# Linear attention and a gated FFN in one kernel: attention pieces issued on a fixed grid of ticks, with FFN matmuls between them

## The chip, the core and the metric

The kernel runs on one core of one Trainium2 chip. The metric is device time in microseconds (us) of one execution. In the profile PE is TensorE's matmuls, PEld its weight loads, DVE VectorE, ACT ScalarE, POOL GpSimd, SP SyncE. POOL and SP also issue the loads and stores. The kernel keeps its tiles in SBUF; its matmuls write to tiles in PSUM, of which it has five for attention (`pa` in the views) and three for the FFN (`pf`).

## The reference, cut to what matters

```python
# batch 8, heads 8, sequence 576, head size 64, 128 features; FFN 512 -> 1536 -> 512
def phi(x):
    proj = einsum('bhsd,df->bhsf', x, w_phi)
    proj = proj - max(abs(proj), axis=-1, keepdims=True)
    return concatenate([exp(proj), exp(-proj)], axis=-1)
q_p, k_p = phi(q), phi(k)
kv  = einsum('bhsf,bhsd->bhfd', k_p, v)
num = einsum('bhsf,bhfd->bhsd', q_p, kv)
den = einsum('bhsf,bhf->bhs', q_p, sum(k_p, axis=2)) + 1e-6
x   = (num / den)                       # heads joined: 4608 tokens x 512
out = (maximum(x @ w_gate, 0) * (x @ w_val)) @ w_out
```

A sequence of 576 is four chunks of 128 rows and 64 more. Both kernels put the last 64 rows of two batches together into one "mixed" tile of 128 rows.

## The kernel before

One attention unit takes two heads of one batch through the whole chain, K and Q together. PE transposes K and Q; DVE copies the result to SBUF; PE projects; DVE takes the maxima; ACT takes the exps; POOL scales v; PE forms kv; PE forms the numerators; DVE combines them; POOL divides; PE transposes the result for the FFN.

```python
def attn_unit(u, qn, kn, vn, mixed, kvs, xT):
    kpm, vs_m = mixed
    # ... (blk: one 128x128 block of K or Q)
    tT = transposed([blk(kn, i) for i in range(4)] + [blk(qn, i) for i in range(4)])
    kps, ek = k_features(tT[:, 0:4], "kp", sb_f)      # PE, DVE max, ACT exps
    vs = sb_f.tile([P, 8, 2, E], BF16, name="vs")
    scale_v(vs, ..., ek, slice(0, P))                 # POOL, two products of 1.04 us
    yield
    # ... q_features: PE, DVE max, ACT exps; cq = exp(2 m)
    yield
    # ... kv: 20 matmuls of 65 columns, ACT copies the result
    yield
    xu = sb_f.tile([P, 8, D], BF16, name="xu")
    for lo, n in GROUPS:                              # 3, 3 and 2 of 8 blocks
        # ... numerators (PE), then finish_rows: DVE t, u, 1/u; POOL x = u/den
    yield
    x_transposed(xu, xT[:, u, :].rearrange("p (c t) -> p c t", t=P))
```

The FFN of the batch before is a second generator. It is advanced by one step for each `yield` of attention. A step is a val and a gate product (8 matmuls) or one output tile (12 matmuls). The program order is only a proposal: the framework's scheduler may reorder the instructions.

```python
for b in range(B):
    # ... loads of the next batch
    ffn = ffn_group(b - 1, xT) if b else iter(())
    xT = sb_x.tile([P, NDC, SF], BF16, name="xT")
    for _ in attention(b, loaded, mix, state, xT):
        next(ffn, None)
    for _ in ffn:
        pass
for g, x in ((B - 1, xT), (B, xT_mix)):
    for _ in ffn_group(g, x):
        pass
```

Of the kernel before, what the change touches and what calls it, by code (L numbers as in the profile page):

```python
# [8 lines left out]
FP32 = mybir.dt.float32  # L9
# [7 lines left out]
def kernel(  # L17
# [16 lines left out]

    nc = tc.nc
# [18 lines left out]
    sb_mix = ctx.enter_context(tc.tile_pool(name="sb_mix", bufs=2))  # L54
    sb_T = ctx.enter_context(tc.tile_pool(name="sb_T", bufs=3))
    sb_f = ctx.enter_context(tc.tile_pool(name="sb_f", bufs=3))
    sb_kv = ctx.enter_context(tc.tile_pool(name="sb_kv", bufs=14))
# [7 lines left out]
    ident = singles.tile([P, P], BF16)  # L65
    make_identity(nc, ident)

    w2 = singles.tile([P, 2, F], BF16)
    nc.vector.memset(w2, 0.0)
    nc.gpsimd.dma_start(out=w2[0:D, 0, :], in_=w_phi)  # L70
    nc.gpsimd.dma_start(out=w2[D : 2 * D, 1, :], in_=w_phi)

    wg_sb = singles.tile([P, NDC, DFF], BF16)
    wv_sb = singles.tile([P, NDC, DFF], BF16)
    wo_sb = singles.tile([P, NFC, DM], BF16)
    xT_mix = singles.tile([P, NDC, SF], BF16)

    vsm = []
    for i in range(2):
        pair = []  # L80
        for bb in range(2):
            t = singles.tile([P, H, 2, E], BF16, name=f"vsm{i}{bb}")
            nc.vector.memset(t[SM * (1 - bb) : SM * (2 - bb)], 0.0)
            pair.append(t)
        vsm.append(pair)
# [8 lines left out]
    def load_batch(b, pieces):  # L94
        qn = sb_in.tile([P, H, C, D], BF16, name="qn")
        kn = sb_in.tile([P, H, C, D], BF16, name="kn")
        vn = sb_in.tile([P, H, C, D], FP32, name="vn")
        step = H // pieces
        for h in range(0, H, step):
            hs = slice(h, h + step)  # L100
            for t, src, eng in ((kn, k, nc.gpsimd), (vn, v, nc.sync), (qn, q, nc.gpsimd)):
                eng.dma_start(
                    out=t[:, hs],
                    in_=src[b, hs, 0:SF, :].rearrange("h (p c) d -> p h c d", c=C),
                )
        return qn, kn, vn

    def load_mixed(i):
        qm = sb_mix.tile([P, H, D], BF16, name="qm")
        km = sb_mix.tile([P, H, D], BF16, name="km")  # L110
        vm = sb_mix.tile([P, H, D], FP32, name="vm")
        for t, src, eng in ((km, k, nc.gpsimd), (vm, v, nc.sync), (qm, q, nc.gpsimd)):
            for bb in range(2):
                eng.dma_start(
                    out=t[SM * bb : SM * (bb + 1)],
                    in_=src[2 * i + bb, :, SF:S, :].rearrange("h p d -> p h d"),
                )
        return qm, km, vm

    def load_weights():  # L120
        nc.gpsimd.dma_start(out=wv_sb, in_=moe_w_val.rearrange("(c p) n -> p c n", p=P))
        nc.gpsimd.dma_start(out=wg_sb, in_=moe_w_gate.rearrange("(c p) n -> p c n", p=P))
        nc.gpsimd.dma_start(out=wo_sb, in_=moe_w_out.rearrange("(c p) n -> p c n", p=P))

    def transposed(blocks):

        pt = psum_a(BF16)
        n = len(blocks)
        for i, blk in enumerate(blocks):
            nc.tensor.matmul(  # L130
                pt[:, P * i : P * i + P], lhsT=blk, rhs=ident, is_transpose=True
            )
        t = sb_T.tile([P, 8, P], BF16, name="tT")
        nc.vector.tensor_copy(  # L134
            t[:, 0:n].rearrange("p a b -> p (a b)"), pt[:, 0 : P * n]
        )
        return t

    def project_rows(T2):

        pp = psum_a()
        for i in range(2):
            nc.tensor.matmul(  # L143
                pp[:, 2 * F * i : 2 * F * (i + 1)],
                lhsT=T2[:, i, :],
                rhs=w2.rearrange("p a f -> p (a f)"),
            )
        return pp

    def row_max(dst, pp):  # L150
        nc.vector.tensor_reduce(  # L151
            dst,
            pp.rearrange("p (c f) -> p c f", f=F),
            axis=AX.X,
            op=ALU.max,
            apply_absolute_value=True,
        )

    def k_features(kT, name, pool):

        mk = sb_s.tile([P, 8], FP32, name="mk")
        kps = []
        for i in range(2):
            pp = project_rows(kT[:, 2 * i : 2 * i + 2])
            row_max(mk[:, 4 * i : 4 * i + 4], pp)
            kp = pool.tile([P, 2, 4, F], BF16, name=f"{name}{i}")
            for s, sign in ((0, 1.0), (1, -1.0)):
                nc.scalar.activation(
                    kp[:, s].rearrange("p c f -> p (c f)"), pp, AF.Exp, scale=sign
                )  # L170
            kps.append(kp)
        ek = sb_s.tile([P, 2, 8], FP32, name="ek")
        for s, sign in ((0, -1.0), (1, 1.0)):
            nc.scalar.activation(ek[:, s, :], mk, AF.Exp, scale=sign)
        return kps, ek

    def scale_v(dst, src, ek, rows):

        for s in range(2):
            e = ek[rows, s, :]  # L180
            nc.gpsimd.tensor_tensor(  # L181
                dst[rows, :, s, 0:D],
                src[rows],
                e[:, :, None].to_broadcast([e.shape[0], 8, D]),
                op=ALU.mult,
            )
            nc.gpsimd.tensor_copy(dst[rows, :, s, D], e)  # L187

    def q_features(qT, m_slices, name):

        for i in range(2):
            pp = project_rows(qT[:, 2 * i : 2 * i + 2])
            row_max(m_slices[i], pp)
        qp = sb_f.tile([P, 2, 2, 4, P], BF16, name=name)
        for par in range(2):
            pf = psum_a()
            nc.tensor.matmul(  # L197
                pf, lhsT=w2[:, par, :], rhs=qT.rearrange("p a b -> p (a b)")
            )
            for s, sign in ((0, 1.0), (1, -1.0)):  # L200
                nc.scalar.activation(  # L201
                    qp[:, s, par].rearrange("p a b -> p (a b)"), pf, AF.Exp, scale=sign
                )
        return qp

    def finish_rows(parts, cq, xu, lo, n):

        t = sb_s.tile([P, 3, E], FP32, name="t")
        u = sb_s.tile([P, 3, E], FP32, name="u")
        r = sb_s.tile([P, 3, 1], FP32, name="r")  # L210
        for rows, pn in parts:
            ab = pn.rearrange("p (c s e) -> p c s e", s=2, e=E)[rows]
            np_ = ab.shape[0]
            nc.vector.tensor_tensor(  # L214
                t[rows, 0:n],
                ab[:, 0:n, 1],
                cq[rows, lo : lo + n][:, :, None].to_broadcast([np_, n, E]),
                op=ALU.mult,
            )
            nc.vector.tensor_tensor(u[rows, 0:n], ab[:, 0:n, 0], t[rows, 0:n], op=ALU.add)  # L220
        nc.vector.reciprocal(r[:, 0:n], u[:, 0:n, D : D + 1])  # L221
        nc.gpsimd.tensor_tensor(  # L222
            xu[:, lo : lo + n],
            u[:, 0:n, 0:D],
            r[:, 0:n].to_broadcast([P, n, D]),
            op=ALU.mult,
        )

    def x_transposed(xu, dst):
        pt = psum_a(BF16)  # L230
        for i in range(4):
            nc.tensor.matmul(  # L232
                pt[:, P * i : P * i + P],
                lhsT=xu[:, 2 * i : 2 * i + 2].rearrange("p a d -> p (a d)"),
                rhs=ident,
                is_transpose=True,
            )
        nc.vector.tensor_copy(dst, pt[:, 0:512].rearrange("p (a b) -> p a b", b=P))

    GROUPS = ((0, 3), (3, 3), (6, 2))  # L240

    def attn_unit(u, qn, kn, vn, mixed, kvs, xT):
        kpm, vs_m = mixed
        blk = lambda t, i: t[:, 2 * u + i // 2, 2 * (i % 2) : 2 * (i % 2) + 2, :].rearrange(
            "p c d -> p (c d)"
        )
        tT = transposed([blk(kn, i) for i in range(4)] + [blk(qn, i) for i in range(4)])
        kps, ek = k_features(tT[:, 0:4], "kp", sb_f)
        vs = sb_f.tile([P, 8, 2, E], BF16, name="vs")
        scale_v(  # L250
            vs, vn[:, 2 * u : 2 * u + 2].rearrange("p h c d -> p (h c) d"), ek, slice(0, P)
        )
        yield
        mq = sb_s.tile([P, 4, 2], FP32, name="mq")
        qp = q_features(tT[:, 4:8], [mq[:, :, hh] for hh in range(2)], "qp")
        cq = sb_s.tile([P, 8], FP32, name="cq")
        nc.scalar.activation(
            cq, mq.rearrange("p c h -> p (c h)"), AF.Exp, scale=2.0
        )
        yield  # L260
# [136 lines left out]
    for b in range(B):  # L397
# [6 lines left out]
        for _ in ffn:  # L404
            pass
# [35 lines left out]
```

## Time and profile before

| | before |
|---|---|
| time | 582.89 us (median of 3, 582.74 to 582.99) |
| span in the profile | 581.4 us |
| PE, DVE, ACT, POOL busy | 77, 48, 43, 30% |
| dense FFN matmuls begin | about 84 us |
| attention ends, FFN alone | from about 520 us |
| one batch in between | 61.9 us |

First the page of before: the busy time of each engine, then three rows of the view in 40 slices (a digit is the busy share of a slice in tenths; PEclk is the granted clock), then the shares of the chain of work that ended last ("issue" is time in which the engine waited for nothing that the profile shows).

```profile
PE 447.6 (77%) x3307; PEld 238.8 (41%) x3368; DVE 280.8 (48%) x681; ACT 248.5 (43%) x573; POOL 176.4 (30%) x317
...
PE   1315669896589788878789698966897788879996
...
POOL 6923322233622332233523222325222222210000
PEclk9999759999999969999899699998899799999999
...
PE 39%; POOL 19%; issue 15%; DVE 10%; ACT 10%; DMA 7%; POOLq 0%; DVEq 0%; another core or an unknown queue 0%; ACTq 0%
```

No engine is full. PE is low at the start, saturated only in the last slices, where the FFN runs alone, and rises and falls in between. Also, PE's busy time overstates its work. The Trainium skill ("Perfetto Trace Analysis", § Identifying the Most-Contended Engine) warns that matmul busy time is no good measure of how close a kernel is to the roofline, because pipelined instructions look smaller in the trace. Here they look longer than the time they take from PE, as the timeline of before shows. Columns: start, length, engine, line, operation, shapes, count.

```profile
308.89 2.75 PE L357 MATMUL pf<-wo_sb,h_3136 128*128 128x512 bf16 x12
```

Twelve matmuls take 2.75 us. Each is recorded with 0.379 us, so they start (2.75 - 0.379) / 11 = 0.2155 us apart. The FFN has 1296 of them, which is 279.5 us. Attention's shorter matmuls, read in the same way, add about 113 us. PE's work is therefore about 393 us of the 581.4.

Next, five rows of the view of waits of before: who waited for whom, us in total, times, longest.

```profile
ACT val_sb L349 <- PE pf L340: 122.5, 68, 6.3
POOL xu L222 <- DVE r L221: 116.8, 46, 5.8
...
PE pa L272 <- POOL vs L187: 55.9, 56, 5.6
...
PE pa L232 <- POOL xu L222: 35.4, 32, 8.0
...
POOL km L114 <- DMA wo_sb<-in_moe_w_out_dram: 6.5, 1, 6.5
```

ACT's and POOL's idle time costs nothing by itself. PE's does: PE stood 55.9 us for the scaled v and 35.4 us for POOL's x. The engines wait for each other in turn.

The pace of a batch is read from the weight loads of the output products, one group per batch. Columns: duration in ns (min/median/max), first and last start in us.

```profile
L357 PEld LDWEIGHTS <-h_1547 x48: 95/98/98, 180.9 to 193.7; 128*128 128x128 bf16 x48
...
L357 PEld LDWEIGHTS <-h_4725 x48: 95/98/98, 428.4 to 441.3; 128*128 128x128 bf16 x48
```

Four batches lie between these two: (428.4 - 180.9) / 4 = 61.9 us per batch. PE's work per batch is about 45.2 us.

### The profile page before, as it was taken

How to read it: one execution, taken by the hardware profiler on the slowest of the kernel's cores; microseconds unless marked ns; L12 is line 12 of the kernel's file. 1: busy time of each engine (PE TensorE's matmuls, PEld its weight loads, DVE VectorE, ACT ScalarE, POOL GpSimd, SP SyncE). 2: the span in 40 equal slices, each digit the busy share in tenths (PEclk: the TensorE clock that was granted, in tenths of full speed). 3: DMA queues.
4: the chain of work that ended last, by engine and by line, in shares of the span. 5: the costliest groups of instructions: out<-in, count | busy, mean ns of one | idle time of the engine just before them, and what ended most of it. 6: DMA issues, size and time to landing. Idle time of an engine off the chain costs nothing.

```text
span 581.4 us, 8833 instructions
## 1 busy us (share of the span) xinstructions
PE 447.6 (77%) x3307; PEld 238.8 (41%) x3368; DVE 280.8 (48%) x681; ACT 248.5 (43%) x573; POOL 176.4 (30%) x317
## 2 busy tenths in 40 slices
PE   1315669896589788878789698966897788879996
PEld 0213444453354444444345344533444444434442
DVE  3213556535664456538563555356543565373140
ACT  2303345534555445444453455345444454432331
POOL 6923322233622332233523222325222222210000
PEclk9999759999999969999899699998899799999999
DMA  9999160029200720082002700270001000100103
GB/s 202 206 203 105 12 135 1 1 62 165 28 1 19 129 72 1 19 163 47 1 1 72 147 0 2 63 156 1 1 19 56 0 2 4 71 1 1 72 1 72
DMA packets 45834, 33.63 MB, mean 58 GB/s; under 512 B 14048, under 2 KB 40160, under 8 KB 45792
## 3 DMA queue, kind: packets, MB, share of 16 engines
q0 software_dynamic: 27952, 14.19, 18.7%
q1 hardware_dynamic: 17840, 18.88, 10.2%
q8 instruction: 26, 0.43, 0.3%
q14 instruction: 16, 0.13, 0.1%
HBM read 37.81 MB, written 9.44 MB: 81 GB/s over the span
## 4 chain that ended last, share of the span: by engine, by line
PE 39%; POOL 19%; issue 15%; DVE 10%; ACT 10%; DMA 7%; POOLq 0%; DVEq 0%; another core or an unknown queue 0%; ACTq 0%
PE pf L340 15%; PE pf L357 12%; POOL vs L181 10%; DMA wo_sb<-in_moe_w_out_dram 5%; PE pa L272 4%; POOL xu L222 3%; DVE u L220 3%; DVE t L214 2%; DVE mk L151 2%; PE pa L232 2%; PE pa L130 2%; DMA kn<-in_k_dram 2%; ACT qp L201 2%; PE pa L143 2%; POOL vs L187 2%
## 5 line engine op out<-in xcount | busy, mean ns | idle before, releaser
L349 ACT CAST val_sb<-pf 128x512 bf16<-128x512 f32 x108 | 64.0, 598 | 129.2 <-PE pf L340 122.5
L340 PE MATMUL pf<-xT,wg_sb 128*128 128x512 bf16 x366 | 107.2, 392 | 5.2 <-ACT val_sb L349 2.7
L340 PE MATMUL pf<-xT,wv_sb 128*128 128x512 bf16 x359 | 110.0, 391 | 1.4 <-issue 0.4
L181 POOL TENSOR_TENSOR vs<-vn,ek 128x512 bf16<-128x512 f32 x64 | 66.8, 1043 | 138.0 <-issue 71.2
L222 POOL TENSOR_TENSOR xu<-u,r 128x192 bf16<-128x192 f32 (+1 forms) x108 | 48.9, 471 | 154.9 <-DVE r L221 116.8
L201 ACT ACTIVATE qp<-pa 128x512 bf16<-128x512 f32 x144 | 75.9, 630 | 19.6 <-PE pa L197 19.4
L214 DVE TENSOR_TENSOR t<-pa,cq 128x195 f32<-128x195 f32 (+3 forms) x120 | 36.7, 327 | 97.2 <-PE pa L286 91.0
L340 PEld LDWEIGHTS <-wg_sb 128*128 128x128 bf16 x432 | 41.8, 101 | 43.5 <-issue 6.8
L143 PE MATMUL pa<-w_96,tT 128*128 128x256 bf16 x288 | 50.1, 308 | 8.8 <-DVE tT L134 7.8
L340 PEld LDWEIGHTS <-wv_sb 128*128 128x128 bf16 x432 | 40.9, 101 | 37.3 <-issue 6.1
L232 PE MATMUL pa<-ident,xu 128*128 128x128 bf16 x144 | 26.1, 240 | 36.4 <-POOL xu L222 35.4
L151 DVE TENSOR_REDUCE mk<-pa 128x4 f32<-128x512 f32 x72 | 46.7, 686 | 14.1 <-PE pa L143 14.1
L365 ACT COPY out_sb<-pf 128x512 f32<-128x512 f32 x36 | 21.4, 593 | 65.9 <-PE pf L357 63.9
L134 DVE COPY tT<-pa 128x1024 bf16<-128x1024 bf16 (+1 forms) x40 | 25.4, 635 | 45.9 <-PE pa L130 45.7
L151 DVE TENSOR_REDUCE mq<-pa 128x4 f32<-128x512 f32 x64 | 41.0, 682 | 3.5 <-PE pa L143 3.5
L143 PEld LDWEIGHTS <-tT 128*128 128x128 bf16 x288 | 28.0, 108 | 32.1 <-DVE tT L134 21.3
L220 DVE TENSOR_TENSOR u<-pa,t 128x195 f32<-128x195 f32 (+3 forms) x120 | 37.2, 332 | 1.7 <-DVE r L221 0.4
L232 PEld LDWEIGHTS <-xu 128*128 128x128 bf16 x144 | 12.4, 104 | 61.4 <-POOL xu L222 58.2
L197 PE MATMUL pa<-tT,w_96 128*128 128x512 bf16 x72 | 29.7, 427 | 0.5 <-DVE mq L151 0.3
L286 PEld LDWEIGHTS <-qp 128*128 128x128 bf16 x512 | 23.7, 107 | 10.8 <-issue 5.4
L277 ACT CAST kv<-pa 128x260 bf16<-128x260 f32 x32 | 12.0, 376 | 35.4 <-PE pa L272 35.4
L286 PE MATMUL pa<-kv,qp 128*128 128x65 bf16 x512 | 24.6, 206 | 3.2 <-ACT kv L277 3.2
(307 smaller groups left out, 628.9 us busy)
## 6 DMA issues: line engine op xcount, KB each, us to landing
out_dram<-out_sb SPq DMA_DIRECT2D x32, 256.0 KB, 2.3
vn<-in_v_dram SPq DMA_DIRECT2D x7, 1024.0 KB, 6.6
kn<-in_k_dram POOLq DMA_DIRECT2D x7, 512.0 KB, 6.7
qn<-in_q_dram POOLq DMA_DIRECT2D x7, 512.0 KB, 8.9
wv_sb<-in_moe_w_val_dram POOLq DMA_DIRECT2D x1, 1536.0 KB, 12.7
wg_sb<-in_moe_w_gate_dram POOLq DMA_DIRECT2D x1, 1536.0 KB, 19.7
wo_sb<-in_moe_w_out_dram POOLq DMA_DIRECT2D x1, 1536.0 KB, 27.1
vm<-in_v_dram SPq DMA_DIRECT2D x8, 128.0 KB, 8.1
```

The source lines that it names most:

```text
L143: nc.tensor.matmul(pp[:, 2 * F * i : 2 * F * (i + 1)], lhsT=T2[:, i, :], rhs=w2.rearrange("p a f -> p (a f)"),)
L151: nc.vector.tensor_reduce(dst, pp.rearrange("p (c f) -> p c f", f=F), axis=AX.X, op=ALU.max, apply_absolute_value=True,)
L181: nc.gpsimd.tensor_tensor(dst[rows, :, s, 0:D], src[rows], e[:, :, None].to_broadcast([e.shape[0], 8, D]), op=ALU.mult,)
L201: nc.scalar.activation(qp[:, s, par].rearrange("p a b -> p (a b)"), pf, AF.Exp, scale=sign)
L214: nc.vector.tensor_tensor(t[rows, 0:n], ab[:, 0:n, 1], cq[rows, lo : lo + n][:, :, None].to_broadcast([np_, n, E]), op=ALU.mult,)
L220: nc.vector.tensor_tensor(u[rows, 0:n], ab[:, 0:n, 0], t[rows, 0:n], op=ALU.add)
L222: nc.gpsimd.tensor_tensor(xu[:, lo : lo + n], u[:, 0:n, 0:D], r[:, 0:n].to_broadcast([P, n, D]), op=ALU.mult,)
L232: nc.tensor.matmul(pt[:, P * i : P * i + P], lhsT=xu[:, 2 * i : 2 * i + 2].rearrange("p a d -> p (a d)"), rhs=ident, is_transpose=True,)
L286: nc.tensor.matmul(pn[:, E * (2 * i + s) : E * (2 * i + s + 1)], lhsT=qp[:, s, c % 2, 2 * hh + c // 2, :], rhs=kv[:, hh, s, :],)
L340: nc.tensor.matmul(ps[name], lhsT=w[:, dc, P * fi : P * fi + P], rhs=xT[:, dc, :], start=(dc == 0), stop=(dc == NDC - 1),)
L349: nc.scalar.copy(val_sb, ps["val"])
L357: nc.tensor.matmul(po, lhsT=h2[:, fi, P * t : P * t + P], rhs=wo_sb[:, fi, :], start=(fi == 0), stop=(fi == NFC - 1),)
```

## The change

The intent is to let PE never wait in steady state. Attention is split into K items (two heads) and Q items (two chunks of 128 tokens, all heads). Each stage of an item is an event at a tick. A tick is a place in the order of issue, not a time. Items start on a grid of four ticks. A stage stands one to four ticks behind the one it needs; only Q's numerators stand five or six behind their exps. Every tick of the steady stretch ends with one FFN slice of four matmuls, 0.86 us. A batch has 36 ticks and an FFN group has 36 slices. The order of issue is then fixed on all engines. Besides, the val and gate weights are loaded in thirds, first loads go k, v, then the rest, the division by the denominator is one instruction per chunk instead of three, and the buffers of K's exps and of the scaled v rise from three to four.

```diff
+    ctx.enter_context(tc.manual_schedule())
...
-    def attn_unit(u, qn, kn, vn, mixed, kvs, xT):
...
+    def k_item(b, u):
+        nonlocal items
+        t0 = GAP * items
+        items += 1
...
+        at(t0, start)                         # transposes, DVE copy
+        at(t0 + 2, k_rows, st, 0)             # projections, max, exps
+        at(t0 + 3, k_rows, st, 1)
+        at(t0 + 4, k_values, st, b, u)        # POOL scales v
+        at(max(t0 + 8, last.get(("km", b // 2), 0)), k_kv, st, b, u)
...
+    def q_item(blocks, cols, chunks):
...
+        at(t0, lambda: q_start(st, blocks()))
+        for i in range(2 * n):
+            at(t0 + 2 + i, q_rows, st, i)
+            ci, slot, lo, par = cols[i]
+            at(t0 + 4 + i, q_cols, st, xs[ci], slot, lo, par)
+        for ci, (batches, place, col, dst) in enumerate(chunks):
+            t1 = t0 + 4 + 2 * n + 3 * ci
+            for j in range(3):
+                at(t1 + 2 + j, q_num, st, xs[ci], j, batches, place, col)
+            at(t1 + 7, lambda x=xs[ci], dst=dst: q_finish(x, dst()))
...
+    t = last["x", 0] + 2
+    for g in range(B + 1):
...
+        for fn in ffn_slices(g):
+            at(t, fn)
+            t += 1
+
+    for _, _, fn, args in sorted(events, key=lambda e: e[:2]):
+        fn(*args)
```

(Comments behind the events are added here. The helpers, the loads and the unchanged arithmetic are cut.)

## The prediction

> **What bounds the kernel now.** No engine is full: the page shows PE 77% busy, DVE 48%, ACT 43%, POOL 30% of 581.4 us. PE's busy time overstates its work: in the timeline twelve 512-column matmuls in a row take 2.75 us, each 0.379 long, so they start 0.2155 us apart. (The Trainium skill, "TensorE: Matmul & The Clock Gate", Part 1, gives 215.7 ns at full clock: the trace agrees.) Read the same way, 128 columns take 0.056, 256 0.109, 65 0.033 us. The 1296 FFN matmuls need 279.5 us, attention's about 113: 393 in all. The other 188 us:
> 1. Start: the timeline has the first dense FFN matmuls at about 84 us. POOL's queue waits for the weights to land (6.5 us each, twice, 31 to 45 us), xu work behind it; batch 0 runs alone.
> 2. Steady state: about 61 us per batch against 45 of PE work. The chain of waits goes round one unit: kT, DVE maximum, ACT exps, POOL v scaling (1.04 us twice), kv, numerator, DVE, POOL xu, PE transposes. A unit's latency alternates with bursts of 12 FFN matmuls instead of overlapping: in the view of waits ACT waits 122 us for val, POOL 117 for r, DVE 91 for numerators.
> 3. Tail: FFN alone from 520 us, PE full.
>
> **The change.** Same matmul work. Each stage of an item comes 1 to 4 ticks after the one it needs, with 4 FFN matmuls (0.86 us) per tick: 36 ticks and 36 slices per batch, so other items cover a wait. Removed: 72 of 108 reciprocals (0.165 us; 12 us of DVE); xu in one piece. Added: smaller transposed copies, 3 us of DVE. First loads go k, v before weights, which come in thirds.
>
> **Cost.** Per tick, averaged over 72: PE 0.864 + 0.393 = 1.26 us; DVE about 1.0, ACT 0.95, POOL 0.46 (durations of the groups by form). PE becomes the bound, nearly all on the critical path. In Q items DVE (8.1 us per two chunks plus 2.7 for h2, per 8 ticks) equals PE's 10.6, so some stalls remain with fixed order and 5 + 3 PSUM buffers: I allow 6% of the mixed stretch.
> - FFN starts at tick 48: data at 10 us, 5 K items at 3.3 us (ACT), 4 Q chunks and 3 K items at DVE's pace (22 us), latency 4: about 53 us.
> - PE work left: 393 - 17 = 376 us; 6% of the mixed 311 us: 19.
> - End (copy, store): 4 to 5; timer over profile: 1.
>
> Predicted 453 us (-22%), 80% range 436 to 485. Faster by over 2%: 0.96; within 2%: 0.02; slower: 0.02.
>
> **In the profile.** First dense FFN at 50 to 56 us. From there to about 375 us PE tenths at 9; batches 47 to 49 us apart; FFN alone for the last 65 us. The chain over 70% PE, "issue" and POOL small. Granted clock of the mixed stretch from 0.93-0.95 to near 1. ACT's idle before val shrinks; DVE's busy falls about 10 us.
>
> **What would make it wrong.** DVE or ACT falling behind in Q items (exps wait for the maximum on the same PSUM tile; four-tick bursts of exps plus val copy exceed a tick), so PE often waits for PSUM buffers: batches of 52 to 55 us, 485 to 505 in all. Batch 1's k and v late behind 3 MB of weights: up to 5 us. Below 440 only if PE runs without gaps and the start is under 45 us.

## The result, and the profile after

| | before | after |
|---|---|---|
| time | 582.82 us (4 runs, 582.37 to 582.99) | 453.3 us (4 runs, 451.44 to 454.26) |
| span in the profile | 581.4 | 452.5 |
| first dense FFN matmul | 84 | 62.1 |
| from there to the end | 497 | 390.4 |
| one batch, steady | 61.9 | 46.35 |

The ratio is 0.7775, with a 95% interval of 0.7749 to 0.78. Ratios here are the mean time of one kernel's runs over that of the other's in the same rounds, so they are not quite the ratio of the medians. Executions over 1.5% slower than the fastest of the same kernel are left out of the means. All outputs are right.

The first dense FFN matmul in the timeline, first of before (six single ones came between 49 and 74 us), then of after:

```profile
84.29 0.63 PE L340 MATMUL pf<-xT,wv_sb 128*128 128x512 bf16 x1
```

```profile
62.08 1.48 PE L314 MATMUL pf<-xT,wv_sb 128*128 128x512 bf16 x3 [0.22 <-issue]
```

The page of after, with the same rows as for before:

```profile
PE 406.7 (90%) x3310; PEld 232.5 (51%) x3368; DVE 281.0 (62%) x634; ACT 247.0 (55%) x557; POOL 158.0 (35%) x202
...
PE   1457589998999999989999999899999998999995
...
POOL 6485471129502840285116501771154012000000
PEclk9978669999999999999999999999999999999999
...
PE 65%; DVE 17%; POOL 6%; issue 5%; ACT 3%; DMA 2%; POOLq 0%; DVEq 0%; ACTq 0%
```

And the view of waits of after:

```profile
POOL xu L287 <- DVE r L285: 147.0, 22, 13.2
ACT val_sb L323 <- PE pf L314: 58.2, 52, 2.1
...
PE pa L220 <- POOL vs L164: 7.0, 7, 4.0
...
PE pa L294 <- POOL xu L287: 6.8, 14, 1.5
```

PE is at 8 or 9 from the sixth slice on, all but the last. Its wait for the scaled v fell from 55.9 to 7.0 us and that for x from 35.4 to 6.8. POOL waits longer for DVE than before, 147.0 us, which costs nothing: it is simply early. The batches follow each other like this:

```profile
L336 PEld LDWEIGHTS <-h_1567 x48: 95/98/98, 140.3 to 154.7; 128*128 128x128 bf16 x48
...
L336 PEld LDWEIGHTS <-h_4599 x48: 95/98/98, 325.7 to 340.1; 128*128 128x128 bf16 x48
```

(325.7 - 140.3) / 4 = 46.35 us per batch, against about 45.2 of work. So of the 129 us won, about 107 lie after the first FFN matmul (497 - 390.4) and about 22 before it.

One thing did not come: DVE's busy time is 281.0 us, as before (280.8).

### The profile page after: what moved, and what is told of

Its sections match the earlier page's. It is cut to its first block, busy times and chain, and to the rows that moved or that the text cites. A ratio compares the mean times of both kernels' runs of the same rounds, so it can differ in the third digit from the quotient of the medians.

```text
span 452.5 us, 8580 instructions
## 1 busy us (share of the span) xinstructions
PE 406.7 (90%) x3310; PEld 232.5 (51%) x3368; DVE 281.0 (62%) x634; ACT 247.0 (55%) x557; POOL 158.0 (35%) x202
## 4 chain that ended last, share of the span: by engine, by line
PE 65%; DVE 17%; POOL 6%; issue 5%; ACT 3%; DMA 2%; POOLq 0%; DVEq 0%; ACTq 0%
PE pf L314 36%; PE pf L336 12%; PE pa L141 5%; PE pa L220 4%; DVE u L282 4%; DVE t L274 4%; PE pa L130 3%; POOL vs L158 3%; DMA km<-in_k_dram 2%; PE pa L265 2%; PE pa L243 2%; POOL xu L287 1%; DVE mk L146 1%; PE pa L294 1%; DVE xT L300 1%
## 5 line engine op out<-in xcount | busy, mean ns | idle before, releaser
L287 POOL TENSOR_TENSOR xu<-u,r 128x512 bf16<-128x512 f32 x36 | 37.5, 1043 | 173.6 <-DVE r L285 147.0
L314 PE MATMUL pf<-xT,wg_sb 128*128 128x512 bf16 x369 | 97.5, 381 | 0.6
L314 PE MATMUL pf<-xT,wv_sb 128*128 128x512 bf16 x365 | 97.0, 381 | 1.0 <-issue 0.2
L323 ACT CAST val_sb<-pf 128x512 bf16<-128x512 f32 x108 | 64.2, 594 | 60.0 <-PE pf L314 58.2
L265 PEld LDWEIGHTS <-qp 128*128 128x128 bf16 x640 | 33.9, 99 | 18.4 <-DVE u L282 1.0
L265 PE MATMUL pa<-kv,qp 128*128 128x65 bf16 x640 | 38.8, 195 | 0.7 <-DVE u L282 0.4
L325 DVE SCALAR_TENSOR_TENSOR h_6189<-pf,val_sb 128x512 bf16<-128x512 f32 x12 | 8.3, 692 | 22.8 <-PE pf L314 22.8
L294 PE MATMUL pa<-ident,xu 128*128 128x128 bf16 x144 | 14.7, 227 | 6.8 <-POOL xu L287 6.8
L225 ACT CAST kv<-pa 128x260 bf16<-128x260 f32 x32 | 12.5, 391 | 13.6 <-PE pa L220 13.6
L130 PE MATMUL pa<-ident,kn 128*128 128x128 bf16 x128 | 14.2, 241 | 5.9 <-POOL ident masks.py:199 5.9
L300 DVE COPY xT<-pa 128x512 bf16<-128x512 bf16 x32 | 13.5, 420 | 9.4 <-PE pa L294 9.3
L325 DVE SCALAR_TENSOR_TENSOR h_5968<-pf,val_sb 128x512 bf16<-128x512 f32 x12 | 8.3, 692 | 15.3 <-PE pf L314 15.3
L130 PEld LDWEIGHTS <-kn 128*128 128x128 bf16 x128 | 9.6, 108 | 7.8 <-DMA kn<-in_k_dram 4.9
```

The costliest lines, as they stand in the source:

```text
L130: nc.tensor.matmul(pt[:, P * i : P * i + P], lhsT=blk, rhs=ident, is_transpose=True)
L265: nc.tensor.matmul(pn[:, E * (2 * i + s) : E * (2 * i + s + 1)], lhsT=x["qp"][:, s, slot, blk, :], rhs=kvs[b, h // 2][:, h % 2, s, :],)
L287: nc.gpsimd.tensor_tensor(x["xu"], x["u"][:, :, 0:D], r.to_broadcast([P, 8, D]), op=ALU.mult)
L294: nc.tensor.matmul(pt[:, P * i : P * i + P], lhsT=x["xu"][:, 2 * i : 2 * i + 2].rearrange("p a d -> p (a d)"), rhs=ident, is_transpose=True,)
L314: nc.tensor.matmul(ps, lhsT=w[:, dc, P * fi : P * fi + P], rhs=xT[:, dc, :], start=(dc == 0), stop=(dc == NDC - 1),)
L323: nc.scalar.copy(st["val"], ps)
```

## The experiments

My theory, called L below: the gain comes from the distance in the order of issue between a stage and the one it needs, filled evenly with FFN matmuls. The rivals: fixing the order is itself the gain (F); only the amount of FFN work counts, not its grain (G); the lags are longer than they need to be; the better loads make the start.

### Is it the fixing of the order?

The first run takes the fixing away from the kernel after, the second gives it to the kernel before.

```diff
 e1_auto_order (after):
-    ctx.enter_context(tc.manual_schedule())
+    pass
 e2_before_fixed (before):
+    ctx.enter_context(tc.manual_schedule())
```

> The kernel after, without the one line that fixes the program's order; the scheduler may reorder again. Compared before the run, only 20 rows of PE's 6739 stand elsewhere, but 273 rows of DVE's order. Theory L (the gain comes from the order in which the pieces are issued, that is the lags of 1 to 4 ticks with an FFN slice in each, which the scheduler here keeps on PE): 450 to 465 us, steady batches 46 to 48 us. Rival F (the fixing of the order on all engines is itself the gain): over 490 us.

> The kernel before, with its program order fixed on all engines and nothing else. Its program puts each stage of a unit right behind the one it needs. Theory L: no gain, 570 to 690 us, since PE now waits in order for each DVE, ACT and POOL stage. Rival F: most of the gain, under 520 us.

Without the fixing the kernel after took 459.34 us (458.63 to 460.0; ratio to before 0.788). With the fixing the kernel before took 632.36 us (one run, state unknown, far outside any change of state that other runs here showed). F falls. The program order of after is already so good that the scheduler leaves PE's order nearly alone. (The comparison of the compiled instruction lists counts a moved row twice: its 20 differing lines on PE are 10 rows.) Fixing is worth about 6 us of 129. In the profiled executions 3.0 of the 4.4 us between the two are there by the first gate matmul (66.4 against 63.4 us), nearly all of them after the first val matmul (62.4 against 62.1). Before's program order is worse, over the whole run, than what the scheduler makes of it.

### The grain of the FFN work

The slices of four ticks are issued together, in the last of the four. The work, the items and the lags counted in ticks stay.

```diff
 e3_bursts (after):
         for fn in ffn_slices(g):
-            at(t, fn)
+            at(t + 3 - t % 4, fn)
             t += 1
```

> The kernel after with the FFN slices of four ticks issued together in the last of the four (16 matmuls in a row, none in three ticks), same work and same lags in ticks. Theory L with grain (a lag covers a wait only if FFN matmuls lie inside it): steady batches 48 to 54 us instead of 46.4, total 465 to 515. Rival G (only the amount of FFN work per batch matters, not the grain): at most 458 us.

Measured: 525.97 us (524.98 to 528.39; ratio to before 0.9028). G falls: the same work in bursts of 16 matmuls gives back 73 of the 129 us. It is 11 us beyond my range. Here are PE's own waits in this run:

```profile
PE pa L141 <- DVE tT L134: 31.2, 50, 2.9
PE pf L314 <- ACT val_sb L323: 13.0, 20, 0.8
PE pa L294 <- POOL xu L287: 10.4, 18, 1.9
```

The largest wait is the projection for the copy of the transposes. It is a lag of two ticks, which holds no FFN matmul when the burst lies elsewhere. The second is new: in a burst PE asks for the next PSUM tile of the FFN before ACT has emptied an older one. The three rows make 54.6 us where the same three make 13.6 in after; PE's waits do not account for the rest of the 73. Where in the four ticks the burst lies was not varied.

The skill's advice ("Perfetto Trace Analysis", § Optimization Strategy) is to interleave regimes with different limits. No run here leaves the interleaving out; the grain matters: 453.3 us with 4 matmuls at a time, 526.0 with 16.

### The length of the lags

The next two runs shorten lags: all of them, most to about half (Q's numerators only from five or six ticks behind their exps to four or five), then only the last of the K item.

```diff
 e4_half_lags (after), K items; Q items and the mixed item alike:
-        at(t0 + 2, k_rows, st, 0)
-        at(t0 + 3, k_rows, st, 1)
-        at(t0 + 4, k_values, st, b, u)
-        at(max(t0 + 8, last.get(("km", b // 2), 0)), k_kv, st, b, u)
+        at(t0 + 1, k_rows, st, 0)
+        at(t0 + 2, k_rows, st, 1)
+        at(t0 + 2, k_values, st, b, u)
+        at(max(t0 + 4, last.get(("km", b // 2), 0)), k_kv, st, b, u)
 e6_kv_lag6 (after):
-        at(max(t0 + 8, last.get(("km", b // 2), 0)), k_kv, st, b, u)
+        at(max(t0 + 6, last.get(("km", b // 2), 0)), k_kv, st, b, u)
```

> The kernel after with the stage lags about halved (K: rows at ticks 1 and 2, v scaling 2, kv 4 instead of 2, 3, 4, 8; Q: rows from 1, columns from 2, numerators 1 to 3 after, finish 4 after), same slices per tick. Theory L: a K item's chain from transposes to kv takes some 6 us, four ticks are 5 us, so PE waits in most items: steady batches 48 to 56 us, total 465 to 530. Rival (the lags are longer than needed, half covers all): 448 to 458.

> The kernel after with one lag changed: kv comes 6 ticks after the start of its K item instead of 8. In the trace of after the scaled v was ready 0.4 to 1.5 us before kv wanted it, and two ticks are about 2.4 us. Theory L: PE waits some 1.0 to 1.9 us in most of the 32 K items, total 480 to 505 us, the view of waits shows 30 to 50 us of PE kv behind POOL's v scaling. Rival (other lags or the amount of FFN work absorb it): at most 460.

Measured: 630.38 us for half lags (629.71 to 635.27; ratio 1.0835), slower than the kernel before by 8%. And 521.39 us with the one lag of kv shortened by two ticks (520.3 to 525.85; ratio 0.8959). Both are beyond my ranges on the slow side, the first by 100 us. Here is PE's wait in the second run, and two of its waits in the first:

```profile
PE pa L220 <- POOL vs L164: 65.4, 31, 4.8
```

```profile
PE pa L220 <- POOL vs L164: 94.2, 31, 4.9
PE pa L294 <- POOL xu L287: 55.8, 32, 7.3
```

With the one short lag PE waits for POOL's scaled v in 31 of 32 K items, 65.4 us in all, where after had 7.0. So this wait grew by 58 us and the time by 68. Some 10 of the 68 us are not in it. I had expected 1.0 to 1.9 us per item, from the slack and the length of two ticks. The mean was 65.4 / 31 = 2.1, with single ones up to 4.8. The skill ("TensorE: Matmul & The Clock Gate", Part 2, step 1) says that only weight loads are pulled ahead on PE and that matmuls stay in program order. This fits: behind a waiting kv matmul PE stood, and FFN slices of the batch before, whose inputs do not come from that kv, stood behind it in its order. While PE stands, it also feeds nothing to DVE and ACT, so that later stages start late. That this is why the waits and the time exceed my sum is argued, not shown.

### Can the kernel before be repaired by its order alone?

In these two runs of before, its pieces are kept and its order is fixed. The units of a batch are staggered: a new one starts every third step. The second run also ends a step after the transposes.

```diff
 e5_before_staggered (before, order fixed):
-        for u in range(NU):
-            yield from attn_unit(u, ...)
-            yield
+        units = [attn_unit(u, ...) for u in range(NU)]
+        step, live = 0, []
+        while units or live:
+            if units and step % 3 == 0:
+                live.append(units.pop(0))
+            live = [g for g in live if next(g, "end") != "end"]
+            step += 1
+            yield
 e7_stagger_split (the same, and in attn_unit):
         tT = transposed(...)
+        yield
         kps, ek = k_features(tT[:, 0:4], "kp", sb_f)
```

> The kernel before with its order fixed (632 us alone) and the units of a batch staggered: a new unit starts every third step, so one or two units are in flight, with one FFN step of 8 or 12 matmuls per step. Pieces are those of before, only their order changes. Theory L (distance in the order is what counts): 520 to 575 us. Rival P (without the split into K and Q pieces nothing is gained, since the waits inside a piece dominate): at least 610 us.

> The staggered kernel before (593 us) with one more break: the step ends after a unit's transposes and their copy, and the projections come one FFN step later. In its trace PE stood 83.5 us in 40 waits for that copy, which sits in the same piece as the projections. Theory L (only waits inside a piece, which no FFN work covers, kept it slow): some 50 to 80 us fall away, 510 to 545 us. Rival (the wait moves to the next stage, since one or two units in flight are too few): at least 575.

Measured: 593.34 us (2 runs, 593.24 to 593.44) and 574.19 us (573.87 to 576.03; ratio to before 0.9859). Staggering takes 39 us off the 632.36 (the run of unknown state), and the extra break 19 more. Against before itself the first is 1.8% slower, which is unclear at the 2% of the verdicts, and the second 1.4% faster, which counts as the same. Both are in the direction of L, and both miss its range; the first lies between the two expectations, the second 0.8 us below the rival's 575. The waits of PE tell why. First with the stagger alone, then with the break:

```profile
PE pa L143 <- DVE tT L134: 83.5, 40, 3.5
PE pa L272 <- POOL vs L187: 19.0, 18, 5.4
PE pa L232 <- POOL xu L222: 11.3, 22, 1.3
```

```profile
PE pa L232 <- POOL xu L222: 43.9, 71, 1.5
PE pa L197 <- ACT kp L168: 24.4, 42, 0.6
PE pa L273 <- POOL vs L187: 21.8, 27, 5.4
...
PE pa L143 <- DVE tT L134: 4.9, 9, 0.8
```

The break did what it should to the wait that it aimed at: 83.5 us became 4.9. But 32.6 us came back at x's transposes and 24.4 at Q's projections. At x's transposes the step waits where the chain is next too long for its distance. The wait of Q's projection is of another kind: it reads only the transposes and weights, so by the program what ACT's exps of K can hold back is its PSUM tile. With a fixed order the number of PSUM tiles is thus a second limit of these two runs, and no run changes it. One covered stage was not enough here.

### The start

My forecast had the first FFN matmul at 53 us; it came at 62.1. The timeline of after shows PE standing in the first K items. Columns as above; in brackets the idle time before, and what ended it.

```profile
14.44 0.59 PE L130 MATMUL pa<-ident,km 128*128 128x128 bf16 x4 [6.44 <-DMA km<-in_k_dram]
...
27.68 0.38 PE L220 MATMUL pa<-vs,kp_212 128*128 128x65 bf16 x4 [3.96 <-POOL vs L164]
```

PE waited 6.44 us for the mixed rows, which stand second in its order. It waited 3.96 us for a scaled v. In that time POOL ended the mixed v, issued two weight slices and then scaled this v; the other two slices came from 27.50 us on, as the wait ended:

```profile
23.80 0.81 POOL L115 DMA_DIRECT2D wv_sb<-in_moe_w_val_dram  x1
24.60 0.76 POOL L115 DMA_DIRECT2D wg_sb<-in_moe_w_gate_dram  x1
...
25.35 2.08 POOL L158 TENSOR_TENSOR vs<-vn,ek 128x512 bf16<-128x512 f32 x2
```

The next runs move the mixed item and the weight slices, then both.

```diff
 s1_km_last (after), and last = {("km", 0): 4 * GAP + 9}:
-            k_item(0, 0)
-            k_item_mixed(0)
-            for u in range(1, NU):
-                k_item(0, u)
+            for u in range(NU):
+                k_item(0, u)
+            k_item_mixed(0)
 s2_weights_later (after):
     t = GAP + 5
+    at(t, load_k, 1)
+    at(t, load_v, 1)
     for i in (1, 2):
-        at(t, load_val_gate, wv_sb, moe_w_val, i)
-        at(t, load_val_gate, wg_sb, moe_w_gate, i)
-        t += GAP
-    at(t, load_k, 1)
-    at(t, load_v, 1)
-    t += GAP
-    at(t, load_q, 1)
-    at(t, load_mixed, 0, "qm", q, nc.gpsimd, BF16)
-    at(t, load_out)
+        at(18 + GAP * i, load_val_gate, wv_sb, moe_w_val, i)
+        at(18 + GAP * i, load_val_gate, wg_sb, moe_w_gate, i)
+    at(30, load_q, 1)
+    at(30, load_mixed, 0, "qm", q, nc.gpsimd, BF16)
+    at(34, load_out)
 s3_both: both edits
 l1_weights_whole (after): NS = 1 instead of 3, load_out() directly behind the
 first weights, so that all three matrices are loaded whole before batch 1's k and v
```

> The kernel after with the first mixed K item moved behind the four K items of batch 0. My forecast of the start (first FFN at 53 us, measured 62) missed by 9 us, nearly all of it in the first K items, where PE stood 6.4 us for the mixed rows to land. If that wait is the cause: first FFN at 56 to 59 us, total 447 to 450. Rival (the start is bound by later data or by DVE): unchanged, 452 to 455.

> The kernel after with the second and third slices of the gate and val weights and the out weights issued 13 ticks later, the loads of batch 1 earlier. If POOL's four weight issues (0.8 us each) between v scalings, where PE waited 4.0 us for scaled v, are the cause of the late start: first FFN at 58 to 60 us, total 449 to 451. Rival (data rate bound): the same or worse, 452 to 458, as the same bytes must land.

> Both edits of the start: mixed K item last among batch 0's K items, and weight slices issued later with batch 1's k and v earlier. Alone they gave 448.8 and 451.3 us. In the first, POOL issued four weight slices between v scalings and PE then stood 7.2 us for batch 1's k and 2.7 us for the scaled mixed v. If those waits are still on the way: first FFN at 52 to 55 us, total 443 to 446. Rival (DVE's pace in batch 0's Q chunks bounds the rest): no better than the first alone, 447 to 450.

> The kernel after with its three weight matrices loaded whole and at once behind batch 0, as in the kernel before. Batch 1's k and v (about 1.5 MB) then land behind 4.5 MB of weights instead of 3. If the load order is a main part of the gain at the start (first FFN at 84 in before, 62 in after): first FFN at 68 to 75 us, total 459 to 466. Rival (the order of the pieces alone sets the start): at most 455.

The time in rounds, the start of the first val matmul and the rest of the span of the profiled execution:

| run | time, us | range | first FFN | rest |
|---|---|---|---|---|
| after | 453.3 | 451.44 to 454.26 | 62.1 | 390.4 |
| l1_weights_whole | 455.47 | 454.32 to 457.88 | 63.5 | 390.7 |
| s2_weights_later | 451.27 | 450.36 to 453.44 | 61.3 | 390.3 |
| s1_km_last | 448.83 | 447.63 to 450.05 | 57.8 | 390.1 |
| s3_both | 445.11 | 443.29 to 448.44 | 51.2 | 390.3 |

The rest is the same to within 0.6 us in all five, so the kernel is two separate problems: a start that ends when batch 0 is through, and a stretch at PE's pace. The start moves with the order of its loads and items. The mixed item alone gives 4.3 us at the first FFN matmul. The later weights alone give 0.8 us, which is less than I expected (only two of the four slices, 1.6 us, stood before the v that PE waited for), and its time overlaps with that of after. Each start is read from one execution, and the executions of one kernel spread by 2 to 5 us, so 0.8 us is not clear of the noise. Together they give 10.9 us. In s1 PE waited elsewhere, as these rows of its waits before 58 us show:

```profile
PE pa L130 <- DMA kn<-in_k_dram: 7.2, 2, 4.3
...
PE pa L220 <- POOL vsm L164: 2.7, 1, 2.7
```

Of the 7.2 us, the timeline puts 4.25 us at 12.26 us, for batch 0's k, and only 2.94 us at 43.97, for batch 1's k, whose load stood behind the weights; my expectation for s3 had put all of it down to batch 1. In s3 the wait for batch 1's k and that for the scaled mixed v are gone, and that for batch 0's k is 2.2 us.

The run with whole weights shows that the loading in thirds is not what made the start shorter: with it undone, the first FFN matmul came only 1.4 us later, of 22. My theory's range of 459 to 466 us fails, and the rival's limit of 455 is met but for half a microsecond. In before, POOL's queue had stood 6.5 us twice, at loads of mixed rows that were issued ahead of x's scaling. The kernel after issues these loads at later ticks, in that run as well. The starts of the runs of before with fixed order bear on this. They keep before's pieces and its whole weights. POOL no longer waits for the weights at these loads, and the first val matmul comes at 74.7 us in e2_before_fixed (state unknown), 69.1 with the stagger and 64.9 with the break as well, against 84.3. So up to 19 of the 22 us come with the order of issue alone. How much of that is the wait of the queue, and how much the order of the pieces, is not separated.

### One more tick where PE still waited

In after's steady stretch, from 110 to 380 us, POOL's x and v were the main waits left: PE's weight loads stood 6.8 us for x, and 2.1 us at kv, where PE itself waited for the scaled v (the view books the 2.1 as issue). So two lags were made one tick longer, on top of both start edits. The FFN still begins at tick 48.

```diff
 s4_both_long (s3_both, and):
-        at(max(t0 + 8, last.get(("km", b // 2), 0)), k_kv, st, b, u)
+        at(max(t0 + 9, last.get(("km", b // 2), 0)), k_kv, st, b, u)
-            at(t1 + 7, lambda x=xs[ci], dst=dst: q_finish(x, dst()))
-            last["q"] = t1 + 7
+            at(t1 + 8, lambda x=xs[ci], dst=dst: q_finish(x, dst()))
+            last["q"] = t1 + 8
-    t = last["x", 0] + 2
+    t = last["x", 0] + 1
```

> The same with two lags one tick longer: kv at 9 instead of 8 ticks, the last transposes at 8 instead of 7 after the chunk's exps; FFN still starts at tick 48. In after's steady stretch (110 to 380 us) PE and its weight loads still stood some 7 us for POOL's xu and 2 us for its scaled v. If that is the residue: 3 to 8 us better than the run with both start edits, 437 to 442. Rival (the lags just cover, PE is at its own pace of about 45.2 us a batch): within 2 us of it.

Measured: 434.46 us (433.23 to 435.44, 5 runs; ratio to before 0.7459, interval 0.7444 to 0.7474). This beats both kernels, after by 4.2%. The gain over s3 is 10.7 us, somewhat more than expected: 7.6 of the 10.1 between the two profiled spans lie in the rest (390.3 to 382.7) and 2.5 in the start. Here is the busy time of PE, PEld, DVE, ACT and POOL between 110 and 380 us, first of s3, then of s4 (behind them the granted clock, the DMA share and GB/s):

```profile
110.00:380.00 270.00, 264.68 (x2303) 152.01 (x2302) 194.16 (x445) 165.15 (x376) 96.14 (x118) 1.00 0.28 60
```

```profile
110.00:380.00 270.00, 269.59 (x2327) 154.89 (x2326) 193.17 (x445) 166.53 (x375) 93.65 (x115) 1.00 0.28 60
```

PE is busy for 269.59 of 270 us, and DVE, ACT and POOL are below 72%. What remains is PE's own work, the start and the end.

## Why the prediction was right or wrong

**The total was right, by two errors that cancel.** The predicted 453 us met the measured 453.3. Its sum had 53 us to the first FFN matmul and 400 us from there to the end. Measured were 62.1 and 390.4, so the first term was 9 us too small and the second 10 us too large. That the total met to 0.3 us is luck; that it lay well inside the range is not.

**Start, mis-sized.** I had "data at 10 us, 5 K items at 3.3 us (ACT)". The first data came at 5 us, but the K items took until 32.4 us, where the first Q transposes ran. That is 26.5 us from the first transposes at 5.9 us instead of 16.5. So 6 of the 9 us are there by 32.4 us, where my sum had 26.5; the other 3 to 4 came in the Q chunks (29.7 us from there to the first FFN matmul, I had 26) and were not traced. I had taken ACT's pace, as if every item's data and POOL's queue were ready. The runs showed in its place the wait for the mixed rows and POOL's queue: with both moved, the first FFN matmul came at 51.2 us, near the 53 of the forecast.

**"6% of the mixed 311 us: 19", mis-sized.** With 376 us of PE work left and 4.8 us from the last matmul to the end, the rest of 390.4 us leaves 9.6 us of stalls, half of what I allowed. That the PE work itself was counted well is shown by s4, whose rest of 382.7 us is 2 us above 376 + 4.8. Batches came 46.35 us apart, not 47 to 49.

**PE becomes the bound: right.** PE's tenths are at 8 or 9, the granted clock is 0.99 to 1.00 from 84 us on (0.89 to 0.98 in the stretches between 84 and 520 us before), the FFN alone takes about the last 70 us (I had 65), and ACT's wait for val fell from 122.5 to 58.2 us. The chain has 65% PE where I said over 70%; "issue" fell from 15 to 5% and POOL from 19 to 6%.

**The mechanism "other items cover a wait": right, but I took it to be more forgiving than it is.** Fixing the order as such is worth 6 us (e1). Grain and lag carry the gain: bursts give back 73 us, two ticks of one lag 68 us, half lags all of it and 48 us more. My experiment ranges for these three were too narrow on the slow side.

**"DVE's busy falls about 10 us": wrong.** It stayed at 281.0 us. The reciprocals did fall, from 17.7 to 7.3 us. But the combining of the numerators rose, as these rows of the costliest groups show, first before, then after (busy us and mean ns stand behind the bar):

```profile
L214 DVE TENSOR_TENSOR t<-pa,cq 128x195 f32<-128x195 f32 (+3 forms) x120 | 36.7, 327 | 97.2 <-PE pa L286 91.0
...
L220 DVE TENSOR_TENSOR u<-pa,t 128x195 f32<-128x195 f32 (+3 forms) x120 | 37.2, 332 | 1.7 <-DVE r L221 0.4
```

```profile
L282 DVE TENSOR_TENSOR u<-pa,t 128x195 f32<-128x195 f32 (+3 forms) x120 | 40.6, 338 | 6.4
...
L274 DVE TENSOR_TENSOR t<-pa,cq 128x195 f32<-128x195 f32 (+3 forms) x120 | 39.5, 329 | 1.1 <-PE pa L265 0.6
```

The same 120 + 120 instructions take 80.1 us in place of 73.9. The timeline shows what changed, first in before, then in after:

```profile
66.33 0.63 DVE L214 TENSOR_TENSOR t<-pa,cq 128x195 f32<-128x195 f32 x2 [4.40 <-PE pa L286]
66.88 0.62 DVE L220 TENSOR_TENSOR u<-pa,t 128x195 f32<-128x195 f32 x2
```

```profile
49.26 0.36 DVE L274 TENSOR_TENSOR t<-pa,cq 128x195 f32<-128x195 f32 x1
49.66 0.36 DVE L282 TENSOR_TENSOR u<-pa,t 128x195 f32<-128x195 f32 x1
```

In before the scheduler had put two t and two u next to each other, and two such neighbours take 0.63 us together although each is 0.35 long: they overlap. In after every u follows its own t and starts only after its end. The mean times of the rows make 79.1 us for the 240 instructions in before and 80.0 in after, so 5 of the 6.2 us are overlap that was lost. I had counted instructions, not what stands next to them. The rest of the 10 us lies in smaller items (the copies of the transposes and the maxima, partly); I did not account for it fully. DVE was not the bound, so it cost nothing.

**What stays open.** How much of the gain needs the split into K and Q items and how much only the lags was not separated: e5 and e7 kept before's pieces and reached 574 us, but with too short distances at other stages, so they say that partial covering is little, not that before's pieces could not be covered. The larger number of buffers for K's exps and the scaled v was not tested alone either. Of the start, 84 to 62 us, the thirds of the weights are excluded and the order of issue alone reached 64.9; which part of the order did it is open. And the 129 us are not all waits: PE's idle time fell by 88 us, but its recorded busy time fell too, by 41 us, for the same matmuls. The higher granted clock is in these 41, and also how closely the matmuls follow each other; the two were not separated.

## What to carry to other kernels

Where one engine should never wait, write the order of issue as a schedule: each stage at a distance from the stage it needs that is a little longer than that stage's chain, with independent work spread evenly inside the distance. Measure the slack of every stage in the trace before you touch it. Two ticks of one lag cost 68 us here and one tick more on two lags gained about 8. No run here tried a lag that is far too long. Treat the start as a problem of its own: its order should follow the arrival of the data.

## What the Trainium skill lacked or had wrong

- "Perfetto Trace Analysis" (§ Optimization Strategy) advises to interleave regimes, without saying how finely. More than half of the gain here hung on the grain: slices of 4 matmuls 453.3 us, the same slices in bursts of 16 526.0 us.
- The same page and section reads consistent bubbles on the engine that should be saturated as a possible lack of SBUF or PSUM. The bubbles here had another cause with the same look: with the same buffers, moving kv by two ticks in the order made 31 waits of PE and 65.4 us out of 7 waits and 7.0 us.
- "TensorE: Matmul & The Clock Gate" (Part 1) gives 215.7 ns between 512-column matmuls when warm; this case agrees (0.2155 us). Part 2 says that only weight loads are pulled ahead; what a waiting matmul then costs in a mixed stream is on no page: 2.1 us per wait in e6_kv_lag6, with FFN matmuls behind it.
- That neighbouring vector instructions can overlap in the trace is not new to the skill. What I found on no page, and would belong to "VectorE: DVE Perf Modes", is what an order with dependent neighbours costs: two 128x195 products side by side took 0.63 us, 0.35 each, and where such pairs were undone, the 240 instructions cost 6.2 us more of DVE's busy time.
